# An attention and expert kernel: weight layout, the head's order and the last unit's tail are changed together

## The chip, the cores and the metric

The kernel runs on one core of one Trainium2 chip. The metric is the device time in microseconds of one execution, lower is better. A time is the median of several executions; a profiled execution has a time of its own, and a span, which runs from its first to its last instruction.

## The reference, cut to what matters

Two layers follow each other. The first is attention with 4 batches, 8 heads, 768 positions and 64 channels a head; a position sees the 8 global keys and the 96 positions up to itself. The second is a mixture of 4 attention experts on the joined heads.

```python
scores = scale * np.matmul(q, k.transpose(0, 1, 3, 2)) + bias
a = softmax(np.where(keep, scores, -1e9))      # keep: global keys, or 0 <= rel < 96
x = np.matmul(a, v)                            # then heads joined: (B, S, 512)
logits = x @ w_gate                            # the two best of 4 experts, softmax over them
for e in range(4):
    y = causal_attention(x @ wq[e], x @ wk[e], x @ wv[e]) @ wo[e]
    out += weight_of_e * y                     # 0 where e isn't among the two best
```

Each of the three weights that x meets, and the gate, is contracted over x's 512 channels.

## The kernel before, in words

The work is cut into 24 units, one for 128 positions of one batch (6 a batch). For each unit three loads of 256 KB bring k, q and v (`load`, line 238, on SP's or ScalarE's DMA queue); `cast` (258) and `cast_v` (267) turn them to half precision on VectorE, GpSimd (POOL) or ScalarE; `turn` (283, 285) transposes k and q on TensorE and copies them out of PSUM. `local_scores` (345, 352, 355) adds the bias by a matmul with an identity, adds the products, and ScalarE takes the exponential; `global_scores` (319 to 328) does the same for the global keys. `global_values` (366) and `local_values` (381) gather into the PSUM tile `zps`; its single buffer is shared with the second layer. Line 388 takes the reciprocal of the sums, and line 390 scales and writes x in half precision. `turn_x` (402, 403) transposes x in 4 pieces of 128 channels, which are the contraction's pieces: `project_qk` (414, 419) and `project_v` (428, 430) multiply piece `ko` of x with row block `ko` of the weights.

The second layer is `causal_scores` (459, 462), `causal_mask` (474, on POOL), `causal_values` (487; 494 to 498 scale by the reciprocal and the expert's weight), `turn_z` (509, 512) and `output` (519, 522, 523), which copies 128 x 512 numbers out of PSUM and stores them. PSUM has the pools `psS` (two double banks, scores), `psZ` (one double bank, z) and `psT` (two single banks, transposes, projections and outputs).

Each engine takes its instructions in the order of a list written out by hand, the string `ORDER` (lines 791 to 830): a slot names a stage, a unit and an engine or queue (`kc0v` casts key 0 on VectorE, `lk1s` loads key 1 by SP, `wm14` issues 14 filler matmuls of 240 columns at line 248, which keep TensorE busy while it has no data). `bias_constants` (85 to 95) is the slot `xb0`; it is the first of VectorE's work and ends with four instructions at line 94 that write the bias tile `biasT`. Weights are loaded by `weights_in` (162, 165; 158 for the gate) and cast by `weights_cast` (174, 178, 182).

After the last unit, `check_sums` (741, 742) counts how many reciprocals lie in a safe range; a matmul with ones adds the counts up (774 to 778). Every engine loads the count (780) and branches (782) over a general path that isn't taken here. `branch_hint` (slot `bh0`) tells three engines of that branch.

Of the kernel before, what the change touches and what calls it, by code (L numbers as in the profile page):

```python
# [18 lines left out]
P = 128  # L19
# [3 lines left out]
def kernel(  # L23
# [59 lines left out]

    def bias_constants(_):
        V.tensor_copy(rel[:, :], rel_i[:, :])
        ge = const.tile([P, W], F32, name="ge")
        V.tensor_scalar(ge[:, :], rel[:, :], 0.0, None, op0=Alu.is_ge)
        lt = const.tile([P, W], F32, name="lt")
        V.scalar_tensor_tensor(lt[:, :], rel[:, :], float(NL), ge[:, :],
                               op0=Alu.is_lt, op1=Alu.mult)  # L90
        V.tensor_scalar(lt[:, :], lt[:, :], -1.0, -NEG, op0=Alu.add, op1=Alu.mult)
        V.tensor_scalar(rel[KB:P, :], rel[KB:P, :], slopes[1] / slopes[0], None, op0=Alu.mult)
        for p in range(NP):
            V.scalar_tensor_tensor(biasT[:, p, :], rel[:, :], -slopes[2 * p] / sc1, lt[:, :],
                                   op0=Alu.mult, op1=Alu.add)
# [57 lines left out]
    def weights_in(i, on):  # L153

        issue = queues[on]
        if i == 4:
            w32s[i] = wst.tile([P, NK, E], F32, name="wg32", tag="wg32", bufs=1)
            issue(w32s[i][:, :, :], moe_w_gate.rearrange("(ko kp) e -> kp ko e", kp=P))
            return
        w32s[i] = wst.tile([P, E, NK, Hd], F32, name="w32", tag="w32")  # L160
        if i < 3:
            issue(w32s[i][:, :, :, :],
                  (moe_wk, moe_wq, moe_wv)[i].rearrange("e (ko kp) d -> kp e ko d", kp=P))
        else:
            issue(w32s[i][:, :, :, :].rearrange("p e k d -> p (e k d)")
                  .rearrange("p (a m) -> p a m", a=NEP),
                  moe_wo.rearrange("(a b) d m -> (b d) a m", b=2))
# [31 lines left out]
    NC, current = 120, {}  # L199
# [33 lines left out]
    s16s, zs_, x16s, routing, zss, zts, tps, ppss, zs2 = ({} for _ in range(9))  # L233
# [7 lines left out]
    def keep_warm(n):  # L241


        alone = "z" not in current
        if alone:
            current["z"] = psZ.tile([P, 2, 4 * P], F32, name="zps", tag="z")
        for _ in range(n):
            mm(current["z"][:, 0, 4 * P - 2 * NC:4 * P].rearrange("r (a n) -> r a n", a=2),  # L248
               lhsT=ident[:, :], rhs=ident[:, 0:NC].unsqueeze(1).to_broadcast([P, 2, NC]),
               start=alone, stop=True, skip_group_check=True)  # L250
            alone = False
# [108 lines left out]
    def global_values(u):  # L360

        ag, vg = ags[u], vgs[u // NT]
        zs_[u] = current["z"] = psZ.tile([P, 2, 4 * P], F32, name="zps", tag="z")
        for hf in range(2):
            r = slice(hf * Dh, hf * Dh + Dh)
            mm(zs_[u][:, hf, 0:HG * VW].rearrange("r (h d) -> r h d", h=HG),  # L366
               lhsT=ag[r, :], rhs=vg[r, :, :],
               start=True, stop=False, skip_group_check=True)

    def local_values(u, i):  # L370


        b, ri = divmod(u, NT)
        assert done[u] > i
        for hq in (2 * i, 2 * i + 1):
            for prev in range(2 if ri else 1):
                for c in range(2):
                    for hf in range(2):
                        r = slice(hf * KB, hf * KB + KB)
                        at = c * (2 * P - KB) + prev * P  # L380
                        mm(zs_[u][:, hf, hq * VW:(hq + 1) * VW],  # L381
                           lhsT=as_[u - prev][r, hq % 2, hq // 2, at:at + P],
                           rhs=held("vbuf", u - prev)[r, c, hq, :], start=False, stop=True,
                           skip_group_check=True)
        if i == 1:
            z4 = zs_[u][:, :, 0:HG * VW].rearrange("r a (h d) -> r a h d", h=HG)
            rinv = rinv1[:, b, ri, :].rearrange("r (a h) -> r a h", a=2)
            V.reciprocal(rinv, z4[:, :, :, Dh])
            x16s[u] = pp.tile([P, 2, HG, Dh], F16, name="x16", bufs=5)
            V.tensor_tensor(x16s[u][:, :, :, :], z4[:, :, :, 0:Dh],  # L390
                            rinv.unsqueeze(3).to_broadcast([P, 2, HG, Dh]), op=Alu.mult)

    def turn_x(u, on):

        xTs[u] = pp.tile([P, NK, P], F16, name="xT", bufs=4)
        x16 = x16s[u][:, :, :, :].rearrange("r a h d -> r (a h d)")
        if on == "s":
            nc.sync.dma_start_transpose(xTs[u][:, :, :], x16)
            return
        x_ps = psT.tile([P, NK, P], F16, name="xps", tag="t")  # L400
        for j in range(NK):
            nc.tensor.transpose(x_ps[:, j, :], x16[:, j * P:(j + 1) * P], ident[:, :])  # L402
        copies[on](xTs[u][:, :, :], x_ps[:, :, :])
# [73 lines left out]
    def causal_values(u, i):  # L477

        b, ri = divmod(u, NT)
        n, a2 = ri + 1, a2s[u]  # L480
        assert done["m", u]
        if i == 0:
            zs2[u] = current["z"] = psZ.tile([P, 2, 4 * P], F32, name="zps2", tag="z")
        z_ps = zs2[u][:, 0, 0:E * VW].rearrange("r (e d) -> r e d", e=E)
        for e in range(i * E // 2, (i + 1) * E // 2):
            for ci in range(n):
                mm(z_ps[:, e, :], lhsT=a2[:, e % 2, (e // 2) * n + ci, :],  # L487
                   rhs=held("v2buf", b * NT + ci)[:, e, :], start=(e == 0 and ci == 0), stop=True,
                   skip_group_check=True)
        if i == 0:  # L490
            return
        assert next(routing[u // NH], "end") == "end"
        rinv = rinv2[:, b, ri, :]
        V.reciprocal(rinv, z_ps[:, :, Hd])
        ce = pp.tile([P, E], F32, name="ce")
        V.tensor_mul(ce[:, :], rinv, wts[u // NH][:, ri % NH, :])
        zss[u] = pp.tile([P, E, Hd], F16, name="zs")
        V.tensor_tensor(zss[u][:, :, :], z_ps[:, :, 0:Hd],  # L498
                        ce[:, :].unsqueeze(2).to_broadcast([P, E, Hd]), op=Alu.mult)

    def turn_z(u, on):
        zts[u] = pp.tile([P, NEP, P], F16, name="zt")
        if on == "s":
            nc.sync.dma_start_transpose(zts[u][:, :, :],
                                        zss[u][:, :, :].rearrange("r e d -> r (e d)"))
            return
        zt_ps = psT.tile([P, NEP, P], F16, name="ztps", tag="t")
# [6 lines left out]
    def output(u, on):  # L514
        b, ri = divmod(u, NT)
        assert 3 in ready
        o_ps = psT.tile([P, D], F32, name="ops", tag="t")
# [5 lines left out]
        dma(out[b, ri * P:(ri + 1) * P, :], o_sb[:, :])  # L523

# [34 lines left out]
    def general_path(ctx):  # L559
# [35 lines left out]

        ident32 = gc.tile([P, P], F32, name="ident32")
# [20 lines left out]
        with tc.For_i(0, B, 1) as b:  # L617
# [43 lines left out]
            for ri in range(NT):  # L661
                l_ps = gp.tile([P, MAXB], F32, name="gs", tag="s", bufs=2)
                for ko in range(NK):
                    mm(l_ps[:, 0:E], lhsT=xT[:, ko, ri * P:(ri + 1) * P],
                       rhs=wvg16[:, ko, E * Hd:E * Hd + E],
# [6 lines left out]
            for e in range(E):  # L672
                for w, dst, nm in ((wq16, qs, "q"), (wk16, ks, "k")):
                    d = gb.tile([Hd, S], F16, name=f"g{nm}T{e}")
                    for c in range(2):
                        p_ps = gp.tile([P, MAXB], F32, name="gs", tag="s", bufs=2)
                        for ko in range(NK):
                            mm(p_ps[0:Hd, 0:S // 2], lhsT=w[:, ko, e // 2, e % 2, :],
# [6 lines left out]
                for ct in range(NT):  # L685
                    p_ps = gp.tile([P, MAXB], F32, name="gs", tag="s", bufs=2)
                    for ko in range(NK):
                        mm(p_ps[:, 0:Hd], lhsT=xT[:, ko, ct * P:(ct + 1) * P],
                           rhs=wvg16[:, ko, e * Hd:(e + 1) * Hd],
# [55 lines left out]
    def branch_hint(_):  # L745

        tc.mark_branch_hint_location("general", hint="LikelyTaken", engines=(
            mybir.EngineType.PE, mybir.EngineType.Activation, mybir.EngineType.DVE))
# [5 lines left out]
        "vs": (select_values,), "xb": (bias_constants,), "xi": (half_identities,),  # L754
# [9 lines left out]
    }  # L764
    for slot in ORDER.split():
        stage, *args = stages[slot[:2]]
        if slot[-1].isalpha():
            args.append(slot[-1])
# [6 lines left out]
    n_f = const.tile([1, 1], F32)  # L775
    V.reduce_sum(n_f[:, :], n_ps[:, :], axis=Ax.X)
    n_i = const.tile([1, 1], I32)
    V.tensor_copy(n_i[:, :], n_f[:, :])
# [13 lines left out]
xb0 lk0s kc0v lq0s az0v az1g lk1s xi0a xs0v xk0g lq1a wm14 tk0 qc0g lv0s kc1g lk2s lq2s lk3a  # L792
wm5 tq0a lq3s xc0g lv1a lv2s lq4s lk4a qc1v lq5s vc0g vx0g wm4 tk1 tq1v xm0v lk5s wm10 sa0 sb0
wm10 vs0 gi0 wi0a wm2 gs0 lk6s kc2v qc2v tk2 tq2v wm3 gs1 lq6s wm7 vg0 kc3g va0 vb0 vc1g vx1v
qc3a sa1 az2g sb1 tk3 tq3v tx0v wi1a vg1 az3g qc4a vc2g kc4g vx2v wm2 va1 wm4 sa2 sb2 vb1 qc5g
gs2 kc5a wc0g tk4 tq4v tx1v az4v lv3s vg2 va2 lv4s vb2 sa3 sb3 tk5 tq5v wm6 tx2v kc6a lq7s wi2a
qc6v wm4 sa4 sa5 tk6 vc3g tq6v pk0 sb4 sb5 wc1v pk1 wm2 gs3 wm2 pq0a vx3v pq1a gi1 vg3 vc4g
# [30 lines left out]
ck0 ck1 ca23 bh0 cb23 za21 tz19v zb21 ou18v cc23 tz20v ma22 za22 zb22 tz21a ou19a ou20v ma23 za23 tz22v  # L828
zb23 ou21a ou22a tz23v ou23a ck2
# [41 lines left out]
```

## Time and profile before

| | us |
|---|---|
| median of 3 runs | 152.31 (150.82 to 152.47) |
| profiled execution, its own time | 152.97 |
| its span | 150.8 |
| TensorE matmul busy | 140.3 |
| VectorE busy | 111.4 |
| ScalarE busy | 108.1 |
| POOL busy | 90.2 |

PE is TensorE's matmuls and PEld its weight loads, DVE is VectorE, ACT is ScalarE, POOL is GpSimd, and SP issues transfers; SPq and ACTq are transfers being issued. Lines of 40 digits cut the span into 40 equal slices of 3.77 us; a digit is the busy share in tenths, 9 standing for 90% or more. A line of waits names the engine and line that waited, what released it, the total in us, how often, and the longest. TensorE's matmuls are pipelined, so a full row of 9 says that it was always at work, not that it was at its peak.

### The profile page before, as it was taken

The page shows a single profiled execution, that of the slowest core. Times are in us where ns is not written, and L with a number is a line of the kernel's source. Part 1 is how long each engine was busy: PE and PEld are TensorE (multiplying, and loading weights), DVE is VectorE, ACT ScalarE, POOL GpSimd, SP SyncE. Part 2 cuts the span into 40 slices and gives each one's busy share as a digit, 9 for nine tenths or more (in the row PEclk, how much of TensorE's full clock was granted, in tenths as well). Part 3 has the DMA queues.
Part 4 walks back from the last instruction along what each step waited for, and adds up shares of the span by engine and source line. Part 5 has one row for each costly group of instructions (what it writes and reads, how often), then busy time and mean ns, then how long its engine had stood idle before and what let it go on. Part 6 is the DMA issues. An engine that isn't in the chain of part 4 may idle for free.

```text
span 150.8 us, 7217 instructions
## 1 busy us (share of the span) xinstructions
PE 140.3 (93%) x3029; PEld 110.2 (73%) x3029; DVE 111.4 (74%) x348; ACT 108.1 (72%) x176; POOL 90.2 (60%) x254
## 2 busy tenths in 40 slices
PE   5799999999999999999978999999999999999760
PEld 4567778887778888878757778888778878786520
DVE  4838676687899887878863987687787777778850
ACT  4027657778576888888638998887977978989640
POOL 7278351568878988797827899136286345463200
PEclk9999999999999999999999999999999999999999
DMA  4999998999999989899899963415221005013462
GB/s 99 280 252 286 276 261 192 254 247 238 277 282 275 245 201 249 189 256 208 231 240 288 301 166 113 116 43 142 74 77 70 4 19 195 24 51 127 155 263 97
DMA packets 85364, 27.77 MB, mean 184 GB/s; under 512 B 82000, under 2 KB 82000, under 8 KB 85328
## 3 DMA queue, kind: packets, MB, share of 16 engines
q1 hardware_dynamic: 62496, 21.51, 56.6%
q10 hardware_dynamic: 22832, 5.77, 17.1%
q8 instruction: 24, 0.39, 1.0%
q14 instruction: 12, 0.10, 0.2%
HBM read 20.98 MB, written 6.29 MB: 181 GB/s over the span
## 4 chain that ended last, share of the span: by engine, by line
PE 74%; DMA 11%; DVE 4%; POOL 3%; ACT 2%; issue 1%; SPq 1%; ACTq 0%; POOLq 0%; DVEq 0%
PE pps L414 14%; PE cps L459 7%; PE vps L428 7%; PE tp L283 7%; PE ops L519 6%; PE zps L487 6%; PE zps L381 6%; PE sps L345 5%; PE zps L248 4%; DMA kf<-in_k_dram 4%; DMA vf<-in_v_dram 4%; PE xps L402 3%; PE sps L352 3%; DMA qf<-in_q_dram 3%; PE zps L366 2%; PE ztps L509 2%
## 5 line engine op out<-in xcount | busy, mean ns | idle before, releaser
L462 ACT ACTIVATE a<-cps 128x1024 f16<-128x1024 f32 (+1 forms) x48 | 42.2, 917 | 8.3 <-PE cps L459 6.6
L355 ACT ACTIVATE abuf<-sps 128x636 f16<-128x636 f32 (+1 forms) x48 | 30.6, 686 | 12.8 <-PE sps L352 10.1
L267 POOL CAST vbuf<-vf 64x256 f16<-64x256 f32 x76 | 31.0, 408 | 8.4 <-DMA vf<-in_v_dram 5.2
L474 POOL TENSOR_SCALAR_AFFINE_SELECT a<-a 128x256 f16<-128x256 f16 x48 | 18.3, 409 | 5.1 <-ACT a L462 4.8
L285 DVE COPY kqT<-tp 128x1024 f16<-128x1024 f16 x23 | 15.7, 688 | 6.6 <-PE tp L283 6.1
L390 DVE TENSOR_TENSOR x<-zps,rinv 128x512 f16<-128x512 f32 x24 | 16.6, 691 | 0.8
L487 PE MATMUL zps<-v2buf,a 128*128 128x65 f16 x336 | 16.0, 193 | 0.6 <-DVE zs L498 0.5
L345 PE MATMUL sps<-biasT,ident 64*64 64x318 f16 (+1 forms) x192 | 14.5, 305 | 1.4 <-ACT abuf L355 1.3
L381 PE MATMUL zps<-vbuf,abuf 64*128 64x65 f16 x704 | 15.5, 189 | 0.0
L258 POOL CAST s16k<-kf 128x512 f16<-128x512 f32 x17 | 10.3, 612 | 8.7 <-DMA kf<-in_k_dram 8.3
L487 PEld LDWEIGHTS <-a 128*128 128x128 f16 x336 | 13.3, 97 | 2.1 <-DVE zs L498 0.9
L381 PEld LDWEIGHTS <-abuf 64*128 64x128 f16 x704 | 14.0, 94 | 1.1 <-issue 0.2
L414 PE MATMUL pps<-xT,wk 128*128 128x128 f16 x192 | 14.7, 219 | 0.0
L414 PE MATMUL pps<-xT,wq 128*128 128x128 f16 x192 | 14.5, 219 | 0.0
L248 PE MATMUL zps<-ident 128*128 128x240 f16 x75 | 12.8, 316 | 1.7 <-POOL ident masks.py:199 1.6
L428 PE MATMUL vps<-wvg,xT 128*128 128x260 f16 x96 | 13.9, 275 | 0.0
L459 PEld LDWEIGHTS <-kq 64*128 64x128 f16 x336 | 9.7, 94 | 5.8 <-issue 4.4
L459 PE MATMUL cps<-kq,kq 64*128 64x128 f16 x240 | 13.8, 218 | 0.0
L519 PE MATMUL ops<-wo,zt 128*128 128x512 f16 x48 | 13.5, 380 | 0.4 <-DVE zt L512 0.4
L352 PE MATMUL sps<-kqT 64*64 64x159 f16 (+2 forms) x384 | 13.8, 223 | 0.0
L258 POOL CAST s16q<-qf 128x512 f16<-128x512 f32 x15 | 9.4, 630 | 5.1 <-DMA qf<-in_q_dram 4.9
L414 PEld LDWEIGHTS <-wk 128*128 128x128 f16 x192 | 11.5, 98 | 0.8
(113 smaller groups left out, 286.4 us busy)
## 6 DMA issues: line engine op xcount, KB each, us to landing
out_dram<-osb SPq DMA_DIRECT2D x24, 256.0 KB, 2.3
qf<-in_q_dram SPq DMA_DIRECT2D x20, 256.0 KB, 5.6
kf<-in_k_dram SPq DMA_DIRECT2D x19, 256.0 KB, 5.7
vf<-in_v_dram SPq DMA_DIRECT2D x17, 256.0 KB, 5.5
vf<-in_v_dram ACTq DMA_DIRECT2D x7, 256.0 KB, 4.7
kf<-in_k_dram ACTq DMA_DIRECT2D x5, 256.0 KB, 4.9
qf<-in_q_dram ACTq DMA_DIRECT2D x4, 256.0 KB, 4.5
w<-in_moe_wk_dram ACTq DMA_DIRECT2D x1, 512.0 KB, 5.3
```

Of the source, the lines that this page charges most:

```text
L248: mm(current["z"][:, 0, 4 * P - 2 * NC:4 * P].rearrange("r (a n) -> r a n", a=2), lhsT=ident[:, :], rhs=ident[:, 0:NC].unsqueeze(1).to_bro ...
L258: copies[on](s16s[nm, u][:, :, :], fs[nm, u][:, :, :])
L267: copies[on](o[hf * KB:(hf + 1) * KB, c, :, 0:Dh], fs["v", u][c * KB:(c + 1) * KB, hf * HG:(hf + 1) * HG, :])
L345: mm(s_ps[o, hh, 0:2 * w].rearrange("r (c n) -> r c n", c=2), lhsT=ident2[r, :], rhs=biasT[r, p, 0:w].unsqueeze(1).to_broadcast([KB, 2, w] ...
L355: S_.activation(as_[u][:, :, g, :].rearrange("r h (c n) -> r h c n", c=2)[:, :, :, 0:w], s_ps[:, :, 0:2 * w].rearrange("r h (c n) -> r h c ...
L381: mm(zs_[u][:, hf, hq * VW:(hq + 1) * VW], lhsT=as_[u - prev][r, hq % 2, hq // 2, at:at + P], rhs=held("vbuf", u - prev)[r, c, hq, :], sta ...
L414: mm(p_ps[:, i, ep, :], lhsT=w[:, ko, ep, :, :].rearrange("r a d -> r (a d)"), rhs=xT[:, ko, :], start=(i == 0 and ep == 0 and ko == 0), s ...
L428: mm(v_ps[:, :], lhsT=xT[:, ko, :], rhs=wvg16[:, ko, :], start=(ko == 0), stop=(ko == NK - 1))
L459: mm(s_ps[:, e2, i, :], lhsT=kqs[b * NT + ci][r, 0, ep, :], rhs=kqs[u][r, 1, ep, :], start=(i == 0), stop=True, skip_group_check=True)
L462: S_.activation(a2[:, :, 4 * c:4 * c + len(part), :], s_ps[:, :, 0:len(part), :], func=Exp, scale=sc2)
L487: mm(z_ps[:, e, :], lhsT=a2[:, e % 2, (e // 2) * n + ci, :], rhs=held("v2buf", b * NT + ci)[:, e, :], start=(e == 0 and ci == 0), stop=Tru ...
L519: mm(o_ps[:, :], lhsT=zts[u][:, ep, :], rhs=wo16[:, ep, :], start=(ep == 0), stop=(ep == NEP - 1))
```

## The change

The diff has these parts.

- **Weights.** wk, wq, wv and the gate are loaded with contraction index `kp * 4 + ko` instead of `ko * 128 + kp`, so that a partition reads 4 neighbouring rows: 1 KB at a time instead of 256 B (gate: 64 B instead of 16 B).
- **x.** To match, line 390's instruction writes x with every fourth channel side by side. A head takes 128 columns of `zps` instead of 65, and reads step by 4 columns. The filler matmuls write their 240 columns in four pieces of 60.
- **First key.** `bias_constants` loses the four instructions of line 94 to a new slot, `xp0`, which stands behind `kc0v`. Key 1 moves from SP's queue to ScalarE's, behind query 1; key 3 moves from ScalarE's to SP's.
- **Fillers.** `wm14` becomes 15, `wm4` ahead of key 1's transposes 11, a `wm10` 7, a `wm2` 4, a `wm3` 2, and one `wm2` goes: 79 in all instead of 75.
- **Tail.** The checks `ck0 ck1` move from before unit 21's scores to behind unit 20's z transposes. The last unit's two halves get a PSUM bank each, and are scaled, transposed and multiplied separately; the output is two halves of 256 columns, copied by VectorE and ScalarE and stored by SP and ScalarE. Last z transposes and outputs use `psS` banks.
- **End.** The count is reduced straight into an integer, one instruction less. The branch hint is given on five engines instead of three, at the head of the list.
- The general path, which isn't taken, loads its own weights.

```diff
-        for p in range(NP):
-            V.scalar_tensor_tensor(biasT[:, p, :], rel[:, :], -slopes[2 * p] / sc1, lt[:, :],
-                                   op0=Alu.mult, op1=Alu.add)
+        const_of["lt"] = lt
+
+    def pair_biases(_):
+        for p in range(NP):
+            V.scalar_tensor_tensor(biasT[:, p, :], rel[:, :], -slopes[2 * p] / sc1,
+                                   const_of["lt"][:, :], op0=Alu.mult, op1=Alu.add)
...
-            issue(w32s[i][:, :, :, :],
-                  (moe_wk, moe_wq, moe_wv)[i].rearrange("e (ko kp) d -> kp e ko d", kp=P))
+            issue(w32s[i][:, :, :, :].rearrange("p e k d -> p e (k d)"),
+                  (moe_wk, moe_wq, moe_wv)[i].rearrange("e (kp ko) d -> kp e (ko d)", ko=NK))
...
-    NC, current = 120, {}
+    NC, current = 60, {}
...
-            mm(current["z"][:, 0, 4 * P - 2 * NC:4 * P].rearrange("r (a n) -> r a n", a=2),
-               lhsT=ident[:, :], rhs=ident[:, 0:NC].unsqueeze(1).to_broadcast([P, 2, NC]),
+            mm(current["z"][:, 0, :].rearrange("r (a n) -> r a n", a=HG)[:, :, P - NC:P],
+               lhsT=ident[:, :], rhs=ident[:, 0:NC].unsqueeze(1).to_broadcast([P, HG, NC]),
...
-            mm(zs_[u][:, hf, 0:HG * VW].rearrange("r (h d) -> r h d", h=HG),
+            mm(zs_[u][:, hf, :].rearrange("r (h d) -> r h d", h=HG)[:, :, 0:VW],
...
-            V.tensor_tensor(x16s[u][:, :, :, :], z4[:, :, :, 0:Dh],
-                            rinv.unsqueeze(3).to_broadcast([P, 2, HG, Dh]), op=Alu.mult)
+            x16s[u] = pp.tile([P, NK, H, Dh // NK], F16, name="x16", bufs=5)
+            V.tensor_tensor(x16s[u][:, :, :, :].rearrange("r k h d -> r h k d"),
+                            z8[:, :, 0:Dh].rearrange("r h (d k) -> r h k d", k=NK),
+                            rinv.unsqueeze(2).unsqueeze(3).to_broadcast([P, H, NK, Dh // NK]),
+                            op=Alu.mult)
...
+        last = u == NU - 1
+        nz = E // 2 if last else E
+        z4 = zs2[u][:, :, 0:nz * VW].rearrange("r a (e d) -> r a e d", e=nz)
...
+        z, e = (z4[:, i], slice(i * nz, i * nz + nz)) if last else (z4[:, 0], slice(0, E))
+        rinv = rinv2[:, b, ri, e]
+        V.reciprocal(rinv, z[:, :, Hd])
...
+    def end_tile(u, first, shape, dtype, name):
+        if u < first:
+            return psT.tile(shape, dtype, name=name, tag="t")
+        return psS.tile(shape, dtype, name=name, tag="s")
...
-        zt_ps = psT.tile([P, NEP, P], F16, name="ztps", tag="t")
+        zt_ps = end_tile(u, NU - 2, [P, NEP, P], F16, "ztps")
...
-        o_ps = psT.tile([P, D], F32, name="ops", tag="t")
+        o_ps = end_tile(u, NU - 3, [P, D], F32, "ops")
...
+    def turn_last_z(ep, on):
+        zt_ps = psT.tile([P, P], F16, name="ztps1", tag="t")
+        nc.tensor.transpose(zt_ps[:, :],
+                            zss[NU - 1][:, 2 * ep:2 * ep + 2, :].rearrange("r e d -> r (e d)"),
+                            ident[:, :])
+        zts[ep, "last"] = pp.tile([P, P], F16, name=f"zt{ep}", bufs=1)
+        copies[on](zts[ep, "last"][:, :], zt_ps[:, :])
+
+    def last_output(ep):
+        b, ri = divmod(NU - 1, NT)
+        if ep == 0:
+            outs["last"] = [pool.tile([P, D // 2], F32, name=f"ops{t}", tag=t)
+                            for pool, t in ((psS, "s"), (psT, "t"))]
+        for i in range(2):
+            c = slice(i * D // 2, (i + 1) * D // 2)
+            o_ps = outs["last"][i][:, :]
+            mm(o_ps, lhsT=zts[ep, "last"][:, :], rhs=wo16[:, ep, c], start=(ep == 0),
+               stop=(ep == NEP - 1), skip_group_check=True)
+        if ep == 0:
+            return
+        for i, (copy, queue) in enumerate(((V.tensor_copy, dma), (S_.copy, S_.dma_start))):
+            c = slice(i * D // 2, (i + 1) * D // 2)
+            o_sb = pp.tile([P, D // 2], F32, name=f"osb{i}", bufs=1)
+            copy(o_sb[:, :], outs["last"][i][:, :])
+            queue(out[b, ri * P:(ri + 1) * P, c], o_sb[:, :])
...
-    n_f = const.tile([1, 1], F32)
-    V.reduce_sum(n_f[:, :], n_ps[:, :], axis=Ax.X)
     n_i = const.tile([1, 1], I32)
-    V.tensor_copy(n_i[:, :], n_f[:, :])
+    with nc.allow_low_precision("whole numbers"):
+        V.reduce_sum(n_i[:, :], n_ps[:, :], axis=Ax.X)
...
-xb0 lk0s kc0v lq0s az0v az1g lk1s xi0a xs0v xk0g lq1a wm14 tk0 qc0g lv0s kc1g lk2s lq2s lk3a
-wm5 tq0a lq3s xc0g lv1a lv2s lq4s lk4a qc1v lq5s vc0g vx0g wm4 tk1 tq1v xm0v lk5s wm10 sa0 sb0
-wm10 vs0 gi0 wi0a wm2 gs0 lk6s kc2v qc2v tk2 tq2v wm3 gs1 lq6s wm7 vg0 kc3g va0 vb0 vc1g vx1v
+bh0 xb0 lk0s kc0v xp0 lq0s az0v az1g xi0a xs0v xk0g lq1a lk1a wm15 tk0 qc0g lv0s kc1g lk2s lq2s
+lk3s wm5 tq0a lq3s xc0g lv1a lv2s lq4s lk4a qc1v lq5s vc0g vx0g wm11 tk1 tq1v xm0v lk5s wm10
+sa0 sb0 wm7 vs0 gi0 wi0a wm4 gs0 lk6s kc2v qc2v tk2 tq2v wm2 gs1 lq6s wm7 vg0 kc3g va0 vb0 vc1g
...
-ck0 ck1 ca23 bh0 cb23 za21 tz19v zb21 ou18v cc23 tz20v ma22 za22 zb22 tz21a ou19a ou20v ma23 za23 tz22v
-zb23 ou21a ou22a tz23v ou23a ck2
+ca23 cb23 za21 tz19v zb21 ou18v cc23 tz20v ck0 ck1 ma22 za22 zb22 tz21a ou19a ou20v ma23 za23
+tz22v tz23v zb23 ou21a ou22a ou23 ty23v ck2 oy23
```

## The prediction

> **What bounds the kernel now.** I read the page first: busy shares and slices, then the windows table, then who waited for TensorE, then the head in the timeline.
>
> ```profile
> PE 140.3 (93%) x3029; PEld 110.2 (73%) x3029; DVE 111.4 (74%) x348; ACT 108.1 (72%) x176; POOL 90.2 (60%) x254
> ...
> PE   5799999999999999999978999999999999999760
> ...
> DMA  4999998999999989899899963415221005013462
> ```
>
> TensorE is full from slice 3 to slice 37 except around slices 21 and 22 (75 to 83 us). The DMA engines are nearly full to slice 23. What can be won lies in the first 10 us, near 79 us and in the last 8 us, unless TensorE's own work shrinks. The windows table (PE, PEld, DVE, ACT, POOL busy, then clock, DMA share, GB/s) agrees:
>
> ```profile
> 10.00:20.00 10.00, 9.95 (x198) 7.37 (x197) 7.45 (x19) 5.60 (x11) 6.42 (x16) 1.00 1.25 280
> 30.00:40.00 10.00, 10.00 (x223) 7.96 (x218) 8.13 (x23) 7.30 (x11) 7.54 (x20) 1.00 1.11 250
> 70.00:80.00 10.00, 8.62 (x205) 7.03 (x203) 7.48 (x22) 5.79 (x11) 5.69 (x16) 1.00 1.01 241
> 140.00:151.00 11.00, 5.07 (x64) 2.83 (x63) 4.77 (x21) 3.75 (x7) 0.77 (x2) 0.97 0.44 165
> ```
>
> The waits of TensorE are few; these are the ones the change touches:
>
> ```profile
> PE sps L345 <- ACT abuf L355: 1.3, 1, 1.3
> PE tp L283 <- DVE s16k L258: 1.1, 1, 1.1
> PE zps L487 <- DVE zs L498: 0.5, 1, 0.5
> PE tp L283 <- POOL s16k L258: 0.2, 1, 0.2
> ```
>
> The timeline of the head (start, duration, engine, line) shows the second of them and its price:
>
> ```profile
> 4.26 1.03 DVE L94 SCALAR_TENSOR_TENSOR biasT<-rel,lt 128x159 f16<-128x159 f32 x4
> 5.21 0.42 DVE L258 CAST s16k<-kf 128x512 f16<-128x512 f32 x1
> ...
> 5.68 0.61 PE L283 MATMUL tp<-ident,s16k 128*128 128x128 f16 x4 [1.09 <-DVE s16k L258]
> ...
> 8.05 0.61 POOL L258 CAST s16k<-kf 128x512 f16<-128x512 f32 x1 [1.96 <-DMA kf<-in_k_dram]
> 9.55 1.55 PE L248 MATMUL zps<-ident 128*128 128x240 f16 x10
> 11.71 1.20 PE L248 MATMUL zps<-ident 128*128 128x240 f16 x10
> ```
>
> The first key landed at 4.0 (its issue at 0.80, 3.2 us to landing) but VectorE cast it at 5.21, behind four bias instructions; TensorE stood idle for 1.1 us. The second key landed at 8.0. Fillers start 0.20 us apart until 10.15, then 0.10: the array ran at half rate to 10.15.
>
> [...]
>
> **The change, part by part.**
>
> *First key cast first.* The four L94 instructions (1.03 us) move behind the cast; it starts at about 4.26 instead of 5.21, the transposes at 4.74 instead of 5.68. L94's result is needed only by line 345 at 11.03, so some 5 us cover it; uncovered it would cost its 1.03. Fifteen fillers at 0.20 run from 1.61 to 4.61, so TensorE no longer idles[...].
>
> *Loads reordered.* Key 1 goes to ScalarE's queue behind query 1, where key 3 was issued (2.04) and landed at 7.66; now key 1 lands at 8.00 instead. So it gains some 0.3 us; value 0 takes its place on SP (8.00 instead of 8.89), key 3 lands at about 12.0 and is cast then (before 11.74). SP has as many loads as before. The query-0 transposes wait for POOL's cast (5.29 plus 0.80) and end near 6.6; eleven fillers, at 0.10 each at full rate, end near 7.8; key 1's cast (7.7 plus 0.61) lets its transposes start near 8.4 (before 8.72), and at full rate the eight take 0.45 instead of 0.83. VectorE's copy of them then starts near 8.97 instead of 9.79: 0.8 us earlier. Ten fillers end near 9.9 and line 345 starts near 10.0 instead of 11.03. Past this VectorE decides: its mask of 2.3 us and two casts follow the copy and release unit 2's transposes, so I carry 0.8, not 1.0.
>
> *Fillers.* 79 instead of 75 in all, of the same 240 columns: eight more ahead of key 1's transposes, hidden under its load, four fewer after. Of these, three stand where TensorE decides: 3 x 0.10 = 0.3 us gained.
>
> *Weights in 1 KB runs.* Queue 10 carried 22832 packets of 256 B in 17.1% of 16 x 150.8 us: 18.1 ns each. Queue 1's 62496 took 56.6%: taking 3328 as 2 KB (24 outputs and wo), these took 89 ns. A 1 KB packet, interpolated, 48 ns. One weight: 2048 x 18.1 / 16 = 2.3 us of all engines, after 512 x 48 / 16 = 1.5. Three save 2.3 us of DMA time between 13 and 32 us. This isn't a gain by itself: it lets the loads keep up with a head 0.8 us ahead (query 5, values 1 to 3 and query 6 were cast within 0.1 us of landing). The gate's 512 packets become 128, nothing. Casts keep their shapes.
>
> *x side by side.* Line 390, 24 x 691 ns. Elements, output type and instruction count are the same; the source steps 16 bytes in PSUM and has one dimension more. From below no change[...]. From above half rate: line 498 does 256 elements of the same kind in 424 ns, so 256 more cost 267 and an element 1.04; half rate is 691 + 512 x 1.04 = 1224 ns. I take no change[...]. The z strides (65 to 128 columns) keep runs of 65 and cost nothing.
>
> *Middle.* TensorE lost 1.3 + 0.3 us at 79 to 80: ScalarE's exponentials stood behind its own load of a value (issued 78.20), whose semaphore waited for a query issued at 73.47, landing at 78.13, 4.7 us later. That query follows an output's issue, which follows TensorE, so most moves along; less backlog could take off 0.4 (between 0 and 1.6).
>
> *Tail.* Two checks (0.96 us on VectorE) move from before unit 21's scaling to after unit 20's z copy: unit 21's zs comes 0.9 earlier, unit 22's only 0.1, because the checks now precede it. The last unit: TensorE waits about 0.7 for the first half's scaling (143.1 to 143.8), runs the second half, outputs 21 and 22, then halves of 0.11 instead of 0.22 us a matmul; the last output needs the bank that output 21's ScalarE copy frees near 145.4. Its transposes then end near 145.9, the z copy 146.2, two matmuls 146.5, the two half copies (0.42 VectorE as line 498's 256 columns, 0.37 ScalarE as its 256-column z copy) 147.0, against 146.9 before. ScalarE issues its half's transfer itself (some 0.4), with nothing behind it but the count's load. Two transfers of half the size land about 0.2 sooner than the 2.3 us before; the count ends with one VectorE instruction less (0.14). Together -0.1, between -0.6 and +0.5.
>
> *Hints.* Three are in the trace already, at 0.8 us; two more cost SP some 0.05 us ahead of the first load. After the last branch all five engines go on within 0.46 to 0.61 us, hinted or not: nothing to win.
>
> Sum: -0.8 -0.3 -0.4 -0.1 = -1.6 us. Against the profiled execution: span 150.8 to 149.2, time 152.97 to 151.4 (2.1 lie outside the span). The median is 0.66 below that execution: 152.31 - 1.6 = 150.7.
>
> **The rivals.**
>
> *Swallowed:* the head's gain is given back because loads decide: ten casts to 48 us came within 0.1 us of their landing, and SP's order is unchanged. Against: weights free 2.3 us of DMA time just there. Then only fillers and tail count, 151.9.
>
> *Slower:* the strided read runs at half rate, +0.53 us on each of 24 evictions. The z tile has one buffer; the next user started 0.08 to 0.5 us after the eviction nine times (70.67 after 70.58, 121.78 after 121.69). Summing what 0.53 exceeds these gaps gives some 2.5 us, VectorE's later work perhaps 0.7 more: 150.7 + 3.2 = 153.9. It decides from about 0.25 us per eviction upward: below, the gaps absorb most.
>
> *More:* the stall near 79 goes wholly and the tail gives 0.5: 149.1.
>
> **How the numbers follow.** My forecast 0.52 (its own range 149.9 to 151.4), swallowed 0.22, slower 0.16, more 0.10. A measurement can tell about 1%, 1.5 us, from no change. Faster than 150.8: 0.36 of the forecast's 0.52 and all of more, 0.46. Slower than 153.8: 0.14. The rest, 0.40, is within. Range 148.9 to 153.6: below it half of more, above it most of slower.
>
> **What would show it.** Key 0's cast near 4.3 and the first transposes near 4.7; fillers at 0.10 before 8; line 345 first at about 10.0; line 390 still at 691 ns (above 940 and the slower rival holds); weight packets of 1 KB near 48 ns; the stall near 79 not longer; the last copy ending 3.9 us before the span's end, as before. If line 345 starts at 10.0 but TensorE waits for casts between 19 and 48 us, the gain was swallowed. If the fillers are still at 0.20 near 7, [...]line 345 starts at about 11.5.

## The result, and the profile after

| | before | after |
|---|---|---|
| median, us | 152.02 (150.82 to 152.47, 4 runs) | 163.5 (162.63 to 164.3, 4 runs) |
| profiled execution, its own time, us | 152.97 | 164.3 |
| its span, us | 150.8 | 161.6 |

The ratio is 1.0767, with a 95% interval of 1.0676 to 1.0857. The kernel became 11.5 us slower; the forecast was 150.7, with a range to 153.6. Ratios leave out executions that are slow for their kernel (about 1.5% or more above its fastest), and the runs of e1 below left too few for a ratio.

The page of the kernel after, its slices (PE busy, DMA busy, GB/s moved) and its two queues of loads and stores (packets, MB, share of 16 engines' span):

```profile
PE   5969939999999899589995999999999999999760
...
DMA  4999999999999999999999995341331004112534
GB/s 104 223 218 233 276 204 220 262 196 224 222 217 225 220 215 187 175 254 195 201 266 226 249 274 149 92 130 47 93 134 47 26 0 157 48 65 88 195 154 164
...
q1 hardware_dynamic: 62112, 21.38, 59.2%
q10 hardware_dynamic: 18368, 5.90, 18.3%
```

The same rows of the kernel before:

```profile
GB/s 99 280 252 286 276 261 192 254 247 238 277 282 275 245 201 249 189 256 208 231 240 288 301 166 113 116 43 142 74 77 70 4 19 195 24 51 127 155 263 97
...
q1 hardware_dynamic: 62496, 21.51, 56.6%
q10 hardware_dynamic: 22832, 5.77, 17.1%
```

The DMA row is as full as before, yet less arrives: in the second slice 223 GB/s instead of 280, later often near 220. Queue 1 carries 384 packets fewer, but the share of a span that is 7% longer rises from 56.6 to 59.2%. The DMA engines are not idle; each packet takes longer. In the packet records those of 256 B take 21.7 ns in the mean instead of 18.2. TensorE is no longer full where loads are dense. Its waits after the change:

```profile
PE sps L351 <- ACT abuf L361: 2.8, 3, 1.8
PE gps L329 <- ACT abuf L361: 2.7, 1, 2.7
...
PE zps L372 <- DVE zs L511: 1.5, 1, 1.5
PE tp L289 <- POOL s16k L264: 1.4, 2, 1.2
```

The engine named is the one that came last. That loads stand behind such waits is told by the chain of work that ended last. First the kernel before, then after:

```profile
PE 74%; DMA 11%; DVE 4%; POOL 3%; ACT 2%; issue 1%; SPq 1%; ACTq 0%; POOLq 0%; DVEq 0%
```

```profile
PE 54%; DMA 25%; POOL 5%; DVE 4%; SPq 4%; ACT 3%; issue 2%; ACTq 0%; POOLq 0%; DVEq 0%
```

In a quarter of the span the chain now runs through a transfer. The windows (PE, PEld, DVE, ACT, POOL busy, then clock, DMA share, GB/s) show where, before and after:

```profile
20.00:30.00 10.00, 9.68 (x234) 7.96 (x230) 7.46 (x18) 7.36 (x14) 4.29 (x11) 1.00 1.09 229
...
60.00:70.00 10.00, 10.00 (x260) 7.76 (x253) 7.94 (x23) 8.37 (x15) 7.87 (x20) 1.00 0.93 214
```

```profile
20.00:30.00 10.00, 7.33 (x151) 6.15 (x150) 5.63 (x14) 5.28 (x10) 4.32 (x10) 0.83 1.00 221
...
60.00:70.00 10.00, 7.41 (x201) 6.17 (x202) 5.46 (x19) 6.59 (x12) 7.05 (x20) 1.00 0.92 184
```

The last key landed at 86.5 us before and at 96.5 after: 10.0 of the 10.8 us by which the span grew. From there to the end it is 64.3 us before and 65.1 after. TensorE's granted clock was 0.83 in the first of these windows after the change; TensorE stood idle there for 2.67 us up to 22.99, and from 24 to 26 us the clock was 0.50. That isn't the cause: e13 below loses as much time with a mean clock of 0.992.

**Theory A.** The change drops `n_f`, a constant of 4 bytes which takes 32 in each partition. All that lies behind the constants moves down 32 bytes, the load buffers too. In the compiled programs they begin at 78336, which is 306 x 256, before the change, and at 78304 after it, 224 above a multiple of 256; each buffer is 2048 bytes, so all of them keep that offset. A packet of 256 B then straddles a multiple of 256. The rival is any other part of the change: the 1 KB packets, the order of the loads, the strided x.

### The profile page after: what moved, and what is told of

Same layout as the page of the kernel before. It is cut to its first block, busy times and chain, and to the rows that moved or that the text cites. A ratio compares the mean times of both kernels' runs of the same rounds, so it can differ in the third digit from the quotient of the medians.

```text
span 161.6 us, 7233 instructions
## 1 busy us (share of the span) xinstructions
PE 144.0 (89%) x3035; PEld 112.1 (69%) x3035; DVE 113.8 (70%) x352; ACT 107.5 (66%) x176; POOL 89.6 (55%) x254
## 3 DMA queue, kind: packets, MB, share of 16 engines
q1 hardware_dynamic: 62112, 21.38, 59.2%
## 4 chain that ended last, share of the span: by engine, by line
PE 54%; DMA 25%; POOL 5%; DVE 4%; SPq 4%; ACT 3%; issue 2%; ACTq 0%; POOLq 0%; DVEq 0%
DMA kf<-in_k_dram 12%; PE pps L423 10%; DMA qf<-in_q_dram 8%; PE cps L468 6%; PE ops L534 5%; PE zps L387 5%; PE vps L437 5%; PE zps L498 5%; DMA vf<-in_v_dram 4%; SPq L244 4%; PE tp L289 4%; PE sps L351 3%; PE xps L411 2%; PE sps L358 2%; PE zps L372 2%
## 5 line engine op out<-in xcount | busy, mean ns | idle before, releaser
L291 DVE COPY kqT<-tp 128x1024 f16<-128x1024 f16 x23 | 15.7, 688 | 10.8 <-PE tp L289 10.5
L351 PE MATMUL sps<-biasT,ident 64*64 64x318 f16 (+1 forms) x192 | 15.2, 317 | 2.8 <-ACT abuf L361 2.8
L387 PE MATMUL zps<-vbuf,abuf 64*128 64x65 f16 x704 | 16.7, 195 | 0.1
L387 PEld LDWEIGHTS <-abuf 64*128 64x128 f16 x704 | 15.1, 97 | 1.4 <-issue 0.6
L358 PE MATMUL sps<-kqT 64*64 64x159 f16 (+2 forms) x384 | 14.6, 232 | 0.0
L468 PE MATMUL cps<-kq,kq 64*128 64x128 f16 x240 | 13.8, 218 | 0.0
L254 PE MATMUL zps<-ident 128*128 128x240 f16 x79 | 12.3, 302 | 1.7 <-POOL ident masks.py:199 1.7
L534 PE MATMUL ops<-wo,zt 128*128 128x512 f16 x46 | 12.9, 380 | 0.0
```

What stands on the lines that cost most here:

```text
L351: mm(s_ps[o, hh, 0:2 * w].rearrange("r (c n) -> r c n", c=2), lhsT=ident2[r, :], rhs=biasT[r, p, 0:w].unsqueeze(1).to_broadcast([KB, 2, w] ...
L387: mm(zs_[u][:, hf, hq * P:hq * P + VW], lhsT=as_[u - prev][r, hq % 2, hq // 2, at:at + P], rhs=held("vbuf", u - prev)[r, c, hq, :], start= ...
L468: mm(s_ps[:, e2, i, :], lhsT=kqs[b * NT + ci][r, 0, ep, :], rhs=kqs[u][r, 1, ep, :], start=(i == 0), stop=True, skip_group_check=True)
L534: mm(o_ps[:, :], lhsT=zts[u][:, ep, :], rhs=wo16[:, ep, :], start=(ep == 0), stop=(ep == NEP - 1))
```

## The experiments

The times of every aligned or shifted version, with the mean over the records of all packets of 256 B:

| run | load buffers, mod 256 | median, us | ratio to before (95%) | 256 B packet, mean ns |
|---|---|---|---|---|
| e1, after, 32 up | 0 | 153.53 | no ratio (152.85 before) | 18.1 |
| e2, before, 32 up | 32 | 164.25 | 1.089 (1.0777 to 1.1003) | 23.0 |
| e3, before, 64 up | 64 | 161.57 | 1.0679 (1.0573 to 1.0784) | 21.2 |
| e4, before, 128 up | 128 | 163.84 | 1.081 (1.0693 to 1.0927) | 22.4 |
| e5, before, loads alone 32 up | 32 | 162.89 | 1.0811 (1.074 to 1.0883) | 23.0 |
| e6, before, the rest 32 up | 0 | 152.62 | 1.0028 (0.9987 to 1.007) | 18.2 |
| e13, before without n_f | 224 | 163.94 | 1.0809 (1.0753 to 1.0864) | 22.3 |

**The place of the buffers (e1 to e4).** An unused constant is added behind `good`; it shifts all that follows.

```diff
     good = const.tile([P, NCHK], F32)
+    pad = const.tile([P, 1], F32, name="pad")    # e1 in after, e2 in before; e3 16 and e4 32 columns
```

> The changed kernel with one unused constant of 4 bytes a partition added, which takes the 32-byte slot that the dropped n_f left; all raw load buffers go back to a multiple of 256 bytes. Theory (alignment): the load buffers' start decides the rate; 256-byte packets go back from about 24 to 18 ns while loads are dense, the loads reach 280 GB/s again, and the time is 149 to 152 us. Rival (load order: key 1 on ScalarE's queue, value 0 earlier): still 162 to 164 us, since the order is kept. Rival (x or z strides, 1 KB weights): still 162 to 164.

> The kernel before with an unused constant of 4 bytes a partition: every load buffer moves by 32 bytes, from 0 to 32 past a multiple of 256; nothing else differs. Alignment: 256-byte packets at 23 to 25 ns while loads are dense, 160 to 165 us. Both rivals: 152 us as before.

> The kernel before with an unused constant of 64 bytes a partition: load buffers start 64 past a multiple of 256. If what counts is a line of 64 bytes: 152 us, packets 18 ns. If it counts that a 256-byte packet begins on a multiple of 256 (or 128): as slow as with 32, 160 to 165 us. Rivals: 152 us.

> The kernel before with an unused constant of 128 bytes a partition: load buffers start 128 past a multiple of 256. If 64 or 128 bytes is the unit: 152 us. If 256 is: 160 to 165 us. Rivals: 152 us.

Four bytes take the loss away from the kernel after, and put it into the kernel before. 64 and 128 lose nearly as much as 32 (the intervals overlap): of the offsets tried only 0 modulo 256 is fast.

**Which tiles (e5, e6).** The pool of the load buffers is moved alone, then only what lies behind it.

```diff
+    pad_r = big.tile([P, 8], F32, name="pad_r")               # e5, ahead of the load buffers
+    pad_p = pp.tile([P, 56], F32, name="pad_p", bufs=1)       # e5, 224 bytes behind them; e6 has 8 columns and no pad_r
```

> The kernel before, in which only the buffers of the k, q and v loads lie 32 bytes higher (a 32-byte pad ahead of them, 224 bytes behind them); every other tile lies as in the kernel before or 256 bytes higher. Theory A (a load whose 256-byte packets don't begin on a multiple of 256 in SBUF takes longer per packet): 160 to 165 us, packets of 256 B at 21 to 23.5 ns mean, about 225 GB/s between 10 and 75 us. Rival (it is the place of the tiles that engines read and write, not of the load buffers): 151 to 154 us and 18 ns.

> The kernel before, in which the tiles behind the load buffers (casts, transposes, x, outputs) lie 32 bytes higher and the load buffers stay on multiples of 256. Theory A: 151 to 154 us, packets at 18 ns, as before. Rival (the engines' tiles decide): 160 us or more.

The slices of e5, then of e6:

```profile
GB/s 112 225 218 218 222 217 203 216 210 205 208 235 223 220 220 202 221 185 262 210 253 231 222 262 244 103 128 17 136 135 4 65 4 99 107 65 68 146 250 140
```

```profile
GB/s 100 282 269 287 274 263 216 256 249 188 274 289 286 250 229 237 260 219 259 247 260 229 303 206 75 136 10 145 98 55 71 4 34 184 24 51 113 173 245 121
```

The load buffers alone do it; the tiles that engines read and write don't.

**The loads by themselves (e11, e12).** A kernel of 72 loads and 24 stores, nothing else.

> Loads alone: the 72 loads of q, k and v, 256 KB each in 256-byte packets, issued on two queues by turns into rotating buffers that begin on multiples of 256 in SBUF, and 24 stores of zeros; the whole computation is left out. Both theories: packets at 18 to 20 ns, 270 GB/s or more while the loads run.

> The same loads and stores, the buffers 32 bytes higher; the whole computation is left out. Theory A (the place of the buffer alone slows a dense stream of such packets): mean 23 to 26 ns, 200 to 230 GB/s, loads 15 to 20 us longer than with buffers on multiples of 256. Rival (the place matters only while engines read and write SBUF beside the loads): the same times within 2 us.

86.75 and 107.52 us. The rate and queue 10, which carries only loads here, on multiples of 256 and then 32 above:

```profile
GB/s 18 246 288 288 288 288 288 288 288 288 288 288 288 288 288 288 288 288 288 288 288 289 288 288 289 288 288 289 288 288 289 295 404 407 406 405 405 408 405 126
...
q10 hardware_dynamic: 37440, 9.44, 49.3%
```

```profile
GB/s 47 244 217 218 218 217 218 217 218 218 218 218 218 218 218 218 217 218 218 218 218 218 217 218 218 218 218 218 217 218 218 218 218 294 409 403 406 406 405 168
...
q10 hardware_dynamic: 37440, 9.44, 56.6%
```

A packet takes 0.493 x 16 x 84.7 us / 37440 = 17.8 ns on multiples of 256 and 0.566 x 16 x 105.7 / 37440 = 25.6 ns off them. These records overlap: at 288 GB/s each of the 16 engines finishes 256 B every 14.2 ns, at 218 GB/s every 18.8 ns. 18.87 MB at 288 instead of 218 GB/s is 65.5 instead of 86.6 us: 21.1, against 20.8 measured. The stores, 2 KB packets out of another tile, run at 405 in both. No computing engine takes part, so the rival of e12 falls. The sources are the same in both kernels and only the destination moved. What inside a transfer takes the longer time, 25.6 instead of 17.8 ns a packet, no run shows.

**The dropped constant by itself (e13).**

```diff
-    n_f = const.tile([1, 1], F32)
-    V.reduce_sum(n_f[:, :], n_ps[:, :], axis=Ax.X)
     n_i = const.tile([1, 1], I32)
-    V.tensor_copy(n_i[:, :], n_f[:, :])
+    with nc.allow_low_precision("whole numbers"):
+        V.reduce_sum(n_i[:, :], n_ps[:, :], axis=Ax.X)
```

> The kernel before with one part of the change alone: the count is reduced straight into the integer, so that the 4-byte tile n_f is gone and all that lies behind the constants is 32 bytes lower, the load buffers too. Theory A: nearly the whole loss comes with this line, 161 to 165 us, packets of 256 B at 21 to 23.5 ns mean. Rival (other parts of the change share in the loss, beside the place of the buffers): under 160 us.

163.94 us, ratio 1.0809 (1.0753 to 1.0864), against 1.0767 for the whole change: this line brings the whole loss.

**What the rest of the change is worth (e7 to e10, e14).** All have the 4-byte pad. e7 takes the weights and x back to before, e8 the tail, e9 both; e10 is e7 with the checks put back, e14 is e10 with one slot moved. The hints, the count in one instruction and the z strides stay new in all of them.

```diff
-ca23 cb23 za21 tz19v zb21 ou18v cc23 tz20v ck0 ck1 ma22 za22     # after, e7
+ck0 ck1 ca23 cb23 za21 tz19v zb21 ou18v cc23 tz20v ma22 za22     # e10
-tz22v tz23v zb23 ou21a ou22a ou23 ty23v ck2 oy23                 # after, e7, e10
+tz22v zb23 tz23v ou21a ou22a ou23 ty23v ck2 oy23                 # e14
```

> The changed kernel with the 4-byte pad (loads on multiples of 256), and with weights in 256-byte runs and x contiguous, as before. Theory B (1 KB weight packets on ScalarE's queue hold the engines 46 ns where an SP packet has 18, and so push back SP's loads): key 5 lands by 20.9 us instead of 22.0, and TensorE's stall of 0.9 us near 22.7 is under 0.3; 151.5 to 153. Rival (the weights' issue comes 2.3 us earlier than before and pushes the loads back whatever their packets): key 5 lands at 21.5 or later and the stall stays above 0.6; 152.5 to 154.5.

> The changed kernel with the 4-byte pad and the tail as before (checks ahead of unit 21's scores, last unit in one piece, all z transposes and outputs in the two psT banks). Theory C (the new tail costs some 0.5 us because the two checks, 0.96 us on VectorE, now stand ahead of unit 22's scaling): from the start of unit 21's second half of value matmuls to the last copy 8.1 us as before, instead of 8.8; 152.5 to 153.5. Rival (the tail as it is loses nothing, the 0.5 us came from the middle): 8.7 or more and no gain, 153.5 or more.

> Of the change, the head and the fillers alone: the changed kernel with the 4-byte pad, weights in 256-byte runs and x contiguous, and the tail as before. Theory D (the head's gain of some 1.0 us lasts to unit 21, as it did with the weights alone undone, 137.7 against 138.8 us, and was lost in the tail): 149.8 to 150.5 us, a ratio of 0.990 to 0.996, unit 21's second half of value matmuls starting near 137.7 and the last copy ending 8.1 us later. Rival (the loads take the gain back in this kernel): 151 to 152 us, ratio 0.998 or more, and that start at 138.4 or later.

> The changed kernel with the 4-byte pad, weights and x as before, and of its tail only the two checks put back ahead of unit 21's scores. Theory C (the moved checks cost the tail its 0.65 us): from unit 21's second half of value matmuls to the last copy 8.0 us or less instead of 8.8, about 0.6 us below the version that differs from it only in the checks, 152.1 to 152.5. Rival (it is the last unit's order, its z transposes ahead of the second half of value matmuls, that costs it): 8.5 or more, no difference.

> The version with the checks put back, and in its tail one slot moved: the second half of the last unit's value matmuls ahead of the transposes of its first half. Theory E (the tail loses its 0.65 us because TensorE waits 1.1 us, in its order, at transposes whose scaling stands behind an output's copy on VectorE, while the second half of value matmuls, some 0.5 us of work, stands ready behind them): from unit 21's second half of value matmuls to the last copy 8.2 to 8.5 us instead of 8.8, and 0.3 to 0.6 us below the version with the checks put back. Rival (the end of the tail is set by VectorE's and ScalarE's copies, whatever TensorE does): 8.7 or more, no difference.

| run | weights, x | tail | median, us (runs) | ratio to before (95%) |
|---|---|---|---|---|
| e7 | as before | new | 152.94 (6) | 1.0133 (1.0086 to 1.0179) |
| e8 | new | as before | 151.38 (14) | 0.9993 (0.9959 to 1.0027) |
| e9 | as before | as before | 151.09 (22) | 0.9994 (0.9966 to 1.0022) |
| e10 | as before | new, checks back | 152.33 (17) | 1.0079 (1.0048 to 1.0111) |
| e14 | as before | e10, second half first | 153.85 (6) | 1.0151 (1.0093 to 1.0208) |

*Theory B*, that 1 KB packets push back SP's loads, isn't settled. In e7 key 5 landed at 20.1 us instead of e1's 22.0 and the stall shrank from 0.92 to 0.23 us, as it expected; but with the same weights key 5 landed at 19.7 in e9, 21.5 in e10 and 22.9 in e14. That is scatter between executions. In time the weights and x make no difference: e8 and e9 have the same ratio.

*Theory D*, that the head's gain lasts, falls: e9 is not faster. Its profile looked as if it were, with unit 21's second half of value matmuls at 136.7 us against 138.8 before and a span of 148.5; but e6, whose list is that of before, reached the point at 136.9 with a span of 148.7.

*Theory C*, that the moved checks cost the tail, falls: from unit 21's second half to the last copy it is 8.14 us in before and e8, 8.13 in e9, 8.78 in e1, 8.80 in e7, and still 8.83 in e10 with the checks back. *Theory E*, that the order of two slots does it, falls as well: 8.81 in e14. What stays is the new last unit with its banks, and in it the traces name the split. The timeline of e14:

```profile
143.20 0.69 DVE L534 COPY osb<-ops 128x512 f32<-128x512 f32 x1 [0.38 <-ACT osb L534]
...
143.80 0.16 DVE L505 RECIPROCAL rinv<-zps 128x2 f32<-128x2 f32 x1
144.00 0.16 DVE L507 TENSOR_TENSOR ce<-rinv,wt 128x2 f32<-128x2 f32 x1
144.19 0.29 DVE L508 TENSOR_TENSOR zs<-zps,ce 128x128 f16<-128x128 f32 x1
...
144.54 0.52 PE L495 MATMUL zps<-v2buf,a 128*128 128x65 f16 x12 [0.96 <-DVE zs L508]
```

The second half's matmuls (144.54), now ahead of the transposes, wait for the first half's scaling too: both halves are one tile, and the matmuls start only when VectorE has read it (144.19 + 0.29), though they write the other bank. That scaling stands behind an output's copy of 0.69 us and takes three instructions. Whether two separate tiles would set the second half free wasn't tried.

No version beat the kernel before by more than its interval.

## Why the prediction was wrong

1. **The step that failed** is the last term of *Tail*: "the count ends with one VectorE instruction less (0.14)". That one line made the kernel 12.3 us slower (e13, 163.94 against 151.67). I counted its instruction and not its tile. The tile held up what lies behind it, and the place of the buffers set the rate of dense loads (218 GB/s instead of 288 in e12 and e11). The forecast put this at nothing: it had no term for where tiles lie.
2. **The range failed with it.** All four cases kept 18.1 ns a packet; after the change it was 21.7. *Swallowed* named the right resource, loads that decide, and I had written that ten casts came within 0.1 us of their landing. I took this for a limit on the gain; it was also how far a slower transfer would reach.
3. **The head was right as an order and wrong as a gain.** In e1, with the buffers in place, its lines are where the forecast put them: the cast at 4.3, the transposes near 4.7, the fillers some 0.11 us apart before 8 (eleven in 1.33 us from 6.66 on), line 345 (now 351) at 10.0. That the fillers would reach this spacing so early was an estimate which no trace of before showed; in its head their records of 0.41 us start 0.20 us apart, from 10.15 those of 0.27 us 0.10 apart. The lines of e1:

```profile
4.34 0.43 DVE L264 CAST s16k<-kf 128x512 f16<-128x512 f32 x1
...
4.83 0.61 PE L289 MATMUL tp<-ident,s16k 128*128 128x128 f16 x4
...
6.66 1.33 PE L254 MATMUL zps<-ident 128*128 128x240 f16 x11
...
10.06 0.33 PE L351 MATMUL sps<-biasT,ident 64*64 64x318 f16 x4
```

   But 11.03, which they were set against, belonged to one execution. e6 has the order of before:

```profile
5.68 0.40 PE L284 MATMUL tp<-ident,s16k 128*128 128x128 f16 x4 [1.09 <-DVE s16k L259]
5.92 0.68 PE L249 MATMUL zps<-ident 128*128 128x240 f16 x5
...
10.15 0.33 PE L346 MATMUL sps<-biasT,ident 64*64 64x318 f16 x4
```

   It has the same idle 1.09 us, yet its first transposes at 5.68 us already ran at full rate (four in 0.40 us, in before 0.61) and the line came at 10.15. Over the seven profiles with the head of before (before, e2 to e6, e13) matmuls were seen at full rate from 5.7 us twice and only from 9.8 to 13.8 five times; in the seven that cast the first key first (after, e1, e7 to e10, e14) from 5.4 to 7.6. So full rate came late in five of seven profiles with the idle stretch and in none of seven without it; in e3 to e5 and e13 the slower second key added idle time (in e5 the waits for POOL's casts of keys came to 2.1 us, in before to 0.2). The forecast took the late full rate of one profile for certain; why two came early no run shows.
4. **The stall near 79 us** (-0.4) was scatter as well. Line 345 lost 1.3 + 0.3 us there in the profile of before; e6, with the same list, lost nothing, e1 and e10 neither, e9 0.6, e7 1.2.
5. **Fillers and head in time:** -1.1 forecast for both; e9, which has both, gives 0.9994 (0.9966 to 1.0022), so a gain of over 0.5 us is excluded. Where the early start goes, which in e9's profile stood 1.0 us ahead of before and 0.1 ahead of e6 at line 345, one profile of each can't say. The two more hints were put at 0.05 us without a trace to show it; the first load was issued at 0.90 us after the change, at 0.80 before.
6. **Tail:** forecast 0.1 us later to the last copy, measured 0.64 later. The way there in three legs, in us; the forecast's are from its own times (143.8 and 147.0, and 0.1 before the 142.75 of the profile):

   | | unit 21's second half to the last unit's first half | from there to its second half | from there to the last copy | sum |
   |---|---|---|---|---|
   | before | 3.98 | 0.47 | 3.69 | 8.14 |
   | forecast | 3.88 | 1.15 | 3.2 | 8.23 |
   | e1 | 4.22 | 1.37 | 3.19 | 8.78 |
   | e10, checks back | 3.98 | 1.67 | 3.18 | 8.83 |

   The last leg was right. The two half transfers landed in 1.8 and 2.0 us in e1, against the 2.3 of 256 KB before; the 0.2 saved was an estimate. Two terms are mis-sized. In the first leg unit 22's scaling, put 0.1 earlier, came 0.24 later, because it stands behind the moved checks; in e1 TensorE waited 0.87 us for it, in before it didn't wait here, but 0.5 us at unit 21's:

```profile
141.76 0.52 PE L498 MATMUL zps<-v2buf,a 128*128 128x65 f16 x12 [0.87 <-DVE zs L511]
```

   In the second leg the split cost 0.90 us, not 0.68. With the checks back the first term goes and the second grows to 1.20: TensorE comes earlier, and the first half's scaling stands behind VectorE's output copy of 0.69. So neither place of the checks saves the tail. Of the 152.33 - 151.09 = 1.2 us between e10 and e9, 0.70 lie in these legs and 0.2 outside the span (2.3 against 2.1 us in the mean of each).
7. **The strided x** kept its time, 691 ns, so the *slower* rival's mechanism falls, though its direction came true by another cause. That it would keep it was my estimate; no row of before has such a read. The matmuls into the wider-stepped `zps` kept theirs too: 189 ns in the median before (line 381) and 191 after (387). Line 390 before and line 397 after the change:

```profile
L390 DVE TENSOR_TENSOR x<-zps,rinv 128x512 f16<-128x512 f32 x24 | 16.6, 691 | 0.8
L397 DVE TENSOR_TENSOR x<-zps,rinv 128x512 f16<-128x512 f32 x24 | 16.6, 691 | 0.8
```

8. **1 KB packets** took 46 ns (median of e1; mean 52.6), interpolated at 48. They saved 1.6 points of queue 10's share (16.0% in e1, 17.6% in e7: 2.4 us, forecast 2.3), and it bought nothing that the times show. The forecast took this for time of the engines, but packet records overlap, as the DMA share of 1.25 in its own windows says.

## What to carry to other kernels

Before costing an edit that adds or drops a tile, see where it moves the load buffers: an unused 4-byte constant was worth 8 to 9% here (e2, e13). Begin the buffers of short-packet loads on a multiple of 256 bytes and keep them there: in e11 and e12 that was 288 GB/s instead of 218. And before a stall of one profile goes into a sum, look at a second execution of the same list: the late full rate and the stall near 79 us, 1.2 of the 1.6 us forecast, were not in the other.

## What the runs showed of the hardware

- A dense stream of 256 B packets into SBUF on two queues ran at 288 GB/s (records of 18.0 ns a packet) into buffers on multiples of 256, and at 218 GB/s (25.7 ns) into buffers 32 bytes higher (e11, e12). In the kernel the offsets 32, 64, 128 and 224 all cost: 23.0, 21.2, 22.4 and 22.3 ns.
- A stream that is off, beside one that lies right, cost little. The weights' buffers lie at 192 modulo 256 in the kernel before. Their 256 B packets took 18.5 to 19.1 ns beside loads that lay right, and the two queues together moved 270 GB/s while the first two weights came. Beside loads 32 bytes off (e5) the same weights took 21.9 to 25.3 ns, at 218 GB/s. In e3 it was the other way about, weights on a multiple beside loads 64 off: 18.1 to 19.1 ns, and 276 to 281 GB/s for the first two.
- A VectorE read of PSUM that steps 16 bytes, with half-precision output, took 691 ns for 512 columns, the same as the contiguous read.
